# The first norm's roots on ScalarE, a memset put behind the head, a product ahead of beta's, and an order planned with instruction fetches, in a four-block attention and FFN kernel

## The chip, the cores and the metric

The kernel runs on one core of a Trainium2 chip. The metric is the device time of one execution in microseconds. The median of 3 runs of the kernel before is 536.74 us (536.57 to 538.55).

## What is computed

The input is 2048 tokens of 512 features in bf16. Four residual blocks follow each other: an infini-attention, a gated FFN, the same attention and the same FFN again, with the same weights in both rounds. Every block starts with a layer norm without weights.

```python
def _layernorm(x, axis=-1, eps=1e-05):
    m = jnp.mean(x, axis=axis, keepdims=True)
    v = jnp.var(x, axis=axis, keepdims=True)
    return (x - m) / jnp.sqrt(v + eps)

# attention: 32 heads of 16, the tokens in N = 4 segments of 512, per segment s
logits = jnp.einsum('bhqd,bhkd->bhqk', qs, ks) * scale + mask     # causal
a_dot = jnp.einsum('bhqk,bhkd->bhqd', _softmax(logits), vs)
pq = phi(qs)                                   # where(t > 0, t + 1, exp(t))
a_mem = einsum('bhld,bhde->bhle', pq, M) / (einsum('bhld,bhd->bhl', pq, z)[..., None] + 1e-06)
o = g * a_mem + (1.0 - g) * a_dot              # g = sigmoid(beta), per head
M = M + einsum('bhld,bhle->bhde', phi(ks), vs)
z = z + einsum('bhld->bhd', phi(ks))

# FFN, F = 1792
_gelu(x @ w_gate) * (x @ w_up) @ w_down

x = x + _A_ref(_layernorm(x), ...)     # then _B_ref, _A_ref, _B_ref
```

## The kernel before

**Tiling.** x stays in SBUF as 16 tiles of 128 tokens by 512 features. The work is cut into 8 steps, k = 0 to 7: four segments of 512 tokens in the first round and four in the second. Step k has an attention (class `Att`) and an FFN (class `Ffn`) on the same 512 tokens. An FFN of one step runs interleaved with the attention of the next, so that TensorE has dense products while ScalarE works off the exponentials. Step 0's attention has no FFN beside it; step 7's FFN has no attention beside it.

**One attention.** The norm makes `xn` (DVE, L670; on POOL now and then) from means and variances (L620/L623) and reciprocal roots (POOL, L651 adds eps, L657 raises to the power -0.5). `xn` is transposed to `xnT`, by a DMA from SP's queue (`turn_later`, L520) or by TensorE and an eviction (`turn_item`, L712 and L544/L545). Products make q, k (`kf`) and v. Heads lie 32 rows apart in pairs, so `kx` holds copies of k with one head of each pair masked to zero (`masked_copies`, L495/L500 and a DMA, L799). Scores go to PSUM (L1086), one exponential of 1024 columns at a time turns them into `pt` on ScalarE (L1589), causal masks follow on POOL or DVE (L1538, L1543, L1548), then a "flush" multiplies `pt` by v (L1115), and DVE transposes, normalises and transposes back (L1134, L1144, L1150, L1157) into `aT`. The product with `wo` is added to x (L1206). That sum feeds the FFN's norm, key `xnTf`, whose output feeds the gate products.

**Head of the program.** Lines 1362 to 1425 are written by hand: statistics of the four x tiles (three by BN_STATS on DVE, tile 3 by two ScalarE passes L1383/L1384), roots on POOL (L1378), `xn` (L670), 16 transposes on TensorE (L722) evicted by ScalarE (L725) and DVE (L727), beta's product and its two exponentials (L1408 to L1410), and the first block of k and q in halves of 256 tokens (`first_k` L1059, `first_q` L1064, evictions L1415 to L1424). Before that TensorE does 12 products on a constant tile (`keep_warm`, L417), and DVE zeroes half of one `kx` buffer (L448).

**What sets the order.** Behind the head, a planner written in Python (`order`, with `Clocks` and `Engine`) puts out every engine's instructions in one order. It holds an assumed time for each engine, assumed costs for each operation, and for DMAs an assumed landing time, `max(t + 1.4 + margin, ...)`, ahead of which nothing that needs the data is put out. Its choices (which engine evicts, when a product is due, how urgent a step is) come from a table of numbers, `POLICY`, and from `STAGES`, which changes the numbers per stretch of 20 us of planned time. Where the planner finds nothing ready for TensorE, it puts out a "fill": a product on the constant tile `warm`. On the chip each engine runs its own list in that order and waits on semaphores.

**Three forms of product.** TensorE is used as one 128x128 array ("whole", L559), as four strips of 32 columns (`product` with `tile_position=(0, 32 * c)`, L554; four matmuls for one product; flushes too have this form), or as four strips of rows (scores). The planner stays in a form as long as it can, since a change of form costs time.

**The steps of the FFN's norm (k = 0, 1, 7 are special).** `BY_PE` names the norms whose transposes go to TensorE: those of the FFNs of steps 0, 1 and 7. `QUICK` names the rows of step 1 where the sum with x and the squares are taken by one DVE pass and one ScalarE pass (L633 to L640). All other norms take the roots for four tiles at once and transpose by DMA.

## Time and profile before

| what | value |
|---|---|
| median of 3 runs | 536.74 us (536.57 to 538.55) |
| the profiled execution | 536.73 us |
| its span (first to last instruction) | 534.8 us |
| instructions in the span | 22313 |
| TensorE matmuls | 9803, busy 526.8 us |
| ScalarE | 544 instructions, busy 433.8 us |
| DVE | 814 instructions, busy 432.7 us |
| POOL | 344 instructions, busy 280.2 us |
| exponentials of the scores, L1589 | 288, 1032 ns each |

The profiled execution's time is 1.9 us longer than its span; the rest lies before the first and after the last instruction shown. PE stands for TensorE, ACT for ScalarE, DVE for VectorE, POOL for GpSimd, SP for the engine whose queue issues most DMAs. A row of a timeline has the start, the busy time, the engine, the line of the kernel, the operation with the tiles out<-in, a count, and in brackets how long the engine was idle before it and what released it. Timeline rows put neighbouring instructions of a group together, so two rows of one engine can overlap.

### The profile page before, as it was taken

The page shows a single profiled execution, that of the slowest core. Times are in us where ns is not written, and L with a number is a line of the kernel's source. Part 1 is how long each engine was busy: PE and PEld are TensorE (multiplying, and loading weights), DVE is VectorE, ACT ScalarE, POOL GpSimd, SP SyncE. Part 2 cuts the span into 40 slices and gives each one's busy share as a digit, 9 for nine tenths or more (in the row PEclk, how much of TensorE's full clock was granted, in tenths as well). Part 3 has the DMA queues.
Part 4 walks back from the last instruction along what each step waited for, and adds up shares of the span by engine and source line. Part 5 has one row for each costly group of instructions (what it writes and reads, how often), then busy time and mean ns, then how long its engine had stood idle before and what let it go on. Part 6 is the DMA issues. An engine that isn't in the chain of part 4 may idle for free.

```text
span 534.8 us, 22313 instructions
## 1 busy us (share of the span) xinstructions
PE 526.8 (99%) x9803; PEld 270.1 (51%) x9803; DVE 432.7 (81%) x814; ACT 433.8 (81%) x544; POOL 280.2 (52%) x344
## 2 busy tenths in 40 slices
PE   8999999999999999999999999999999999999997
PEld 4544454555545455545444554545555456545444
DVE  7898899899999998688897889888786797786342
ACT  5999999997998799998999899998879977820320
POOL 4876767385836587337671697816465254100000
PEclk9999999999999999999999999999999999999999
DMA  8345910640122143210130130220231003100001
GB/s 271 67 116 113 242 33 2 171 76 18 34 49 44 24 52 61 43 32 4 43 80 1 26 82 4 42 52 12 63 63 23 1 12 92 24 4 31 11 0 39
DMA packets 72403, 28.83 MB, mean 54 GB/s; under 512 B 56690, under 2 KB 72306, under 8 KB 72306
## 3 DMA queue, kind: packets, MB, share of 16 engines
q1 hardware_dynamic: 72016, 27.15, 23.5%
q8 instruction: 76, 1.25, 1.0%
q10 hardware_dynamic: 290, 0.26, 0.1%
q14 instruction: 21, 0.17, 0.1%
HBM read 9.70 MB, written 2.10 MB: 22 GB/s over the span
## 4 chain that ended last, share of the span: by engine, by line
PE 89%; DVE 5%; ACT 4%; issue 1%; POOL 1%; ACTq 0%; DVEq 0%; POOLq 0%
PE ps L559 43%; PE ps L554 30%; PE ps L1086 8%; PE ps L1115 6%; ACT pt L1589 2%; DVE st L620 1%; DVE gel_sb L1277 0%; ACT wd_sb L545 0%; PE ps L1015 0%; DVE x_sb L1206 0%; DVE byq L1134 0%; DVE e L894 0%; DVE st L1368 0%; DVE xn L670 0%; PE ps L712 0%
## 5 line engine op out<-in xcount | busy, mean ns | idle before, releaser
L1589 ACT ACTIVATE pt<-ps 128x1024 bf16<-128x1024 f32 x288 | 280.3, 1032 | 35.6 <-PE ps L1086 27.2
L1538 POOL TENSOR_SCALAR_AFFINE_SELECT pt<-pt 128x256 bf16<-128x256 bf16 (+1 forms) x192 | 113.9, 606 | 126.5 <-ACT pt L1589 123.1
L1277 DVE TENSOR_TENSOR gel_sb<-gel_sb,ps 128x512 bf16<-128x512 bf16 x112 | 75.6, 683 | 35.6 <-PE ps L559 25.3
L559 PE MATMUL ps<-xnT,wg_sb 128*128 128x512 bf16 x279 | 65.5, 380 | 0.0
L559 PE MATMUL ps<-xnT,wu_sb 128*128 128x512 bf16 x269 | 62.0, 379 | 0.0
L913 POOL TENSOR_SCALAR e<-e 128x512 bf16<-128x512 bf16 x37 | 58.0, 1569 | 2.6 <-ACT e L890 2.0
L1134 DVE STREAM_TRANSPOSE byq<-ps 128x512 f32<-128x512 f32 x64 | 45.3, 707 | 15.5 <-PE ps L1115 14.3
L559 PE MATMUL ps<-wd_sb,gel_sb 128*128 128x512 bf16 (+1 forms) x289 | 56.8, 347 | 0.0
L1206 DVE TENSOR_TENSOR x_sb<-x_sb,ps 128x512 bf16<-128x512 bf16 (+1 forms) x65 | 41.1, 641 | 19.1 <-PE ps L559 15.0
L554 PE MATMUL ps<-wd_sb,gel_sb 128*32 128x512 bf16 (+1 forms) x860 | 49.9, 368 | 0.2 <-issue 0.2
L1543 POOL TENSOR_SCALAR_AFFINE_SELECT pt<-pt 64x1024 bf16<-64x1024 bf16 x28 | 33.4, 1195 | 16.8 <-ACT pt L1589 15.8
L554 PE MATMUL ps<-xnT,wg_sb 128*32 128x512 bf16 x676 | 41.5, 380 | 0.2 <-ACT xnT L545 0.2
L554 PE MATMUL ps<-xnT,wu_sb 128*32 128x512 bf16 x716 | 41.1, 379 | 0.1
L559 PEld LDWEIGHTS <-wg_sb 128*128 128x128 bf16 x279 | 25.7, 98 | 29.7 <-issue 0.9
L559 PEld LDWEIGHTS <-wu_sb 128*128 128x128 bf16 x269 | 25.2, 98 | 29.8 <-issue 0.7
L620 DVE BATCH_NORM_STATS2 st<-x_sb 128x6 f32<-128x512 bf16 x57 | 38.4, 673 | 0.3
L559 PEld LDWEIGHTS <-gel_sb 128*128 128x128 bf16 x289 | 26.8, 98 | 23.2 <-issue 0.9
L1115 PE MATMUL ps<-pt,vaug 128*32 128x256 bf16 (+2 forms) x1344 | 34.8, 238 | 0.0
L544 DVE CAST gel_sb<-ps 128x512 bf16<-128x512 f32 x42 | 28.4, 681 | 6.7 <-PE ps L559 4.0
L1115 PEld LDWEIGHTS <-vaug 128*32 128x32 bf16 x1344 | 27.8, 97 | 10.5 <-issue 1.6
L1336 ACT ACTIVATE gel_sb<-gel_sb 128x2048 bf16<-128x2048 bf16 (+3 forms) x22 | 32.3, 1540 | 0.0
L1086 PEld LDWEIGHTS <-kx 32*128 32x128 bf16 x1120 | 16.6, 92 | 29.0 <-issue 28.4
(152 smaller groups left out, 871.6 us busy)
## 6 DMA issues: line engine op xcount, KB each, us to landing
vz<-vaug SPq DMA_DIRECT2D x14, 136.0 KB, 2.6
wg_sb<-in_B_w_gate_dram SPq DMA_DIRECT2D x8, 224.0 KB, 4.1
wu_sb<-in_B_w_up_dram SPq DMA_DIRECT2D x8, 224.0 KB, 6.4
wd_sb<-in_B_w_down_dram SPq DMA_DIRECT2D x7, 256.0 KB, 4.6
x_sb<-in_A_x_dram SPq DMA_DIRECT2D x3, 512.0 KB, 6.8
out_dram<-x_sb SPq DMA_DIRECT2D x12, 128.0 KB, 1.8
xnT<-xn SPq DMA_TRANSPOSE x48, 2.6
kx<-kf SPq DMA_DIRECT2D x12, 64.0 KB, 2.6
```

Of the source, the lines that this page charges most:

```text
L554: nc.tensor.matmul(out[r], lhsT=lhsT[:, r], rhs=rhs, start=start, stop=stop, tile_position=(0, 32 * c))
L559: nc.tensor.matmul(out, lhsT=lhsT, rhs=rhs, start=start, stop=stop)
L620: nc.vector.bn_stats(out=self.st6[:, 0, :], in_=x_sb[:, self.tt0 + j, :])
L913: lambda eng: eng.tensor_scalar(out=e[0][:], in0=e[0][:], scalar1=1.0, scalar2=None, op0=ALU.min), summed)
L1086: nc.tensor.matmul(ps_all[:, bank, o + c0:o + c0 + n], lhsT=lhsT, rhs=self.q[rows, b, q0:q0 + n], start=True, stop=True, tile_position=(32 ...
L1115: nc.tensor.matmul(ps()[32 * j:32 * j + 32, q0:q0 + nq], lhsT=va[:, ki * VW + g:ki * VW + g + 32], rhs=pt_all[:, places[t], j, o:o + nq], ...
L1134: nc.vector.transpose(out=(self.byq[:, pars[0], :, :].rearrange("p a c -> p (a c)") if h is None else self.byq[:].rearrange("p u a c -> p ...
L1206: ck.dve.post(ck.made(), slack, (0.15 + 0.00104 * (c1 - c0), lambda: nc.vector.tensor_tensor(out=xt, in0=xt, in1=ps()[:, 0:c1 - c0], op=AL ...
L1277: ck.dve.post(ck.made(), NORMAL, (0.683, lambda: nc.vector.tensor_tensor(out=g, in0=g, in1=ps()[:], op=ALU.mult), lambda t: (ps.read(t), e ...
L1538: nc.gpsimd.affine_select(out=view, in_=view, pattern=[[0, 4], [0, n], [1, C]], compare_op=ALU.is_ge, fill=0.0, base=C, channel_multiplier=-1)
L1543: nc.gpsimd.affine_select(out=view, in_=view, pattern=[[0, 4 * TPS], [1, C]], compare_op=ALU.is_ge, fill=0.0, base=0, channel_multiplier=-1)
L1589: nc.scalar.activation(out=pt_all[:, s0:s0 + 2, 2 * p:2 * p + 2, :].rearrange("p r h c -> p h r c"), in_=ps_all[:, pair[0]:pair[1] + 1, :] ...
```

## The change

It has four parts.

1. **The head.** ScalarE now sums and squares x tile 0 instead of tile 3. The reciprocal roots are made by ScalarE, `Ln` with eps as its bias and `Exp` with scale -0.5, for tiles 0 to 2 at once and for tile 3; the two adds of eps on DVE and the two powers on POOL go. A call loads the table set that has both functions. The memset of `kx` leaves the head and is handed to the planner as a job from 12 us on. The turns go to PSUM banks 0, 3, 5, 6, are evicted by ScalarE and DVE alternately, and have one 256-wide product on `warm` between two of them. The first half block of k comes ahead of beta's product, and beta's two exponentials come behind the evictions of the first k and q. The load of x tiles 4 to 7 comes ahead of the second halves of wk and wq.
2. **The norms.** The roots can go to POOL as before, or to ScalarE as `Ln` and `Exp`; the planner chooses. Roots may be taken for pairs of rows (`paired`). The tables `BY_PE` and `QUICK` are replaced by policy numbers (`turn_pe`, `turn_last`, `quick`, `f_urge`) for all FFN norms.
3. **The planner.** It counts TensorE's instructions (`Products`, `issue`) and adds a stall where a chunk of 256 of them would be used up before the next is there, 3.7 us after it was asked for. The landing of a DMA is modelled (`landing`) with a margin of 0.5 us instead of 2.0. Assumed overlaps of ACT and DVE and some assumed costs are new.
4. **The numbers.** `POLICY` is new, and `STAGES` has 13 entries instead of 3. Loads of weights get their times from it.

```diff
+CHUNK, CHUNK_ASKED, CHUNK_END, FETCH = 256, 178, 222, 3.7
...
-BY_PE = {("xnTf", 0), ("xnTf", 1), ("xnTf", NK - 1)}
-QUICK = {("xnTf", 1): (0, 1, 2)}
...
 POLICY = dict(
-    flush_wait=4.959, piece_slack=35.752, kb_slack=40.713, mem_slack=-52.285, margin=2.0, qk_due=1.503, e_q=-1.996,
...
+    rs_pool=2.183, f_urge=-172.366, quick=0, paired=2, turn_pe=1, turn_last=0, w_at=31.878, w_gap=1.658,
...
+    margin=0.5, qk_due=0.997, e_q=-0.936, e_k=1.44, exp_slack=-54.603, e_slack=89.377, phi_slack=25.941,
...
-        self.act, self.dve, self.pool, self.sp = Engine(0.09), Engine(0.07), Engine(), Engine()
+        self.act, self.dve, self.pool, self.sp = Engine(0.118), Engine(0.075), Engine(), Engine()
...
+    def issue(self):
+
+        at = self.issued
+        self.issued += 2.0054
+        if (at - CHUNK_ASKED) // CHUNK != (self.issued - CHUNK_ASKED) // CHUNK:
+            self.asked.append(self.pe)
+        elif (at - CHUNK_END) // CHUNK != (self.issued - CHUNK_END) // CHUNK:
+            late = max(0.0, self.fetched - self.pe)
+            self.stalls += [self.pe] * int(late / 0.05)
+            self.pe += late
+            self.fetched = self.asked[-1] + FETCH if self.asked else 0.0
+
+    def landing(self, t):
+
+        got = max(t + 1.2, self.dma + 1.2)
+        for a in self.asked[-3:]:
+            if -0.6 < a + 1.1 - t < 1.1:
+                got = max(got, a + 2.3 + (1.5 if a + 1.1 < t + 0.1 else 1.1))
+        return got
...
-load_x(1)
+        if not cols.start:
+            load_x(1)
...
-    nc.vector.memset(kxs[1][:, :, :, C:3 * C], 0.0)
...
+    ck.dve.post(12.0, pol.zero_slack, (Port(0.95), lambda: nc.vector.memset(kxs[1][:, :, :, C:3 * C], 0.0),
+                                       lambda t: ev.update({("zero", 1): t})))
...
     def turn_later(t, slack, out, in_, landed, margin=0.0):
 
+        def there(t2):
+            t3 = ck.landing(t2) + margin
+            ck.at(t3 - 0.2, lambda: landed(t3))
+
         def told(t2):
-            t3 = max(t2 + 1.4 + margin, ck.dma + 1.2)
-            ck.at(t3 - 0.2, lambda: landed(t3))
+            ck.at(t2, lambda: there(t2))
...
+            def moved(on_pool):
+                self.ve = wrk.tile([P, n, 1], F32, tag=f"lnve{n}", name="ve")
+                var_in = self.mv[:, j0:j0 + n, var:var + 1]
+                if on_pool:
+                    nc.gpsimd.tensor_scalar(out=self.ve[:], in0=var_in, scalar1=EPS_LN, scalar2=None, op0=ALU.add)
+                else:
+                    nc.scalar.activation(out=self.ve[:], in_=var_in, func=ACT.Ln, bias=eps[:])
...
+            taken = []
+            slack = min(self.urge(j0), URGENT)
+            ck.pool.post(ready, slack + pol.rs_pool, (0.25, lambda: moved(True), None), (1.05, second, told), taken=taken)
+            ck.act.post(ready, slack, (0.29, lambda: moved(False), None), (0.29, power, told), table="exp", taken=taken)
...
         def by_pe(self):
-            return self.key in BY_PE or self.key[0] == "xnTa" and self.key[1] <= pol.pe_turns
+            return (pol.turn_last if self.key[1] == NK - 1 else pol.turn_pe) if self.wide else self.key[1] <= pol.pe_turns
...
     def first_scale(j0, j1):
-        nc.gpsimd.tensor_tensor(out=n0.rs[:, j0:j1, :], in0=n0.mv[:, j0:j1, 1:2], in1=mhalf[:, 0:j1 - j0, :], op=ALU.pow)
+        nc.scalar.activation(out=logs[:, j0:j1, :], in_=n0.mv[:, j0:j1, 1:2], func=ACT.Ln, bias=eps[:])
+        nc.scalar.activation(out=n0.rs[:, j0:j1, :], in_=logs[:, j0:j1, :], func=ACT.Exp, scale=-0.5)
...
+    for j in range(TPS):
+        n0.first_turn(j)
+        if j < TPS - 1:
+            keep_warm(1, 4, 2)
...
+    a0.first_k(ps1, 0, half)
+    te.matmul(beta_ps, lhsT=warm[0:1, :], rhs=beta_row[:], start=True, stop=True)
+    a0.first_q(ps2, 0, half)
...
-    ck.pe, ck.act.free, ck.dve.free, ck.pool.free, ck.sp.free = 10.6, 11.1, 11.0, 8.1, 7.6
+    ck.pe, ck.act.free, ck.dve.free, ck.pool.free, ck.sp.free = 9.3, 9.9, 9.95, 8.0, 7.6
```

Since the planner sets the order, the diff doesn't show where instructions go. Three places follow, with the rows of the engine's list before and after.

The first is DVE's list in the head. `kx` is the buffer that is zeroed, `st` and `mv` are the statistics, `xn` is the normed tile. Before:

```order
L448 MEMSET kx_121 128x16x64
L1368 BN_STATS st_144<-x_sb 128x6
L1368 BN_STATS st_145<-x_sb 128x6
L1371 BN_AGGR mv<-st_144 128x2
L1371 BN_AGGR mv<-st_145 128x2
L1374 TENSOR_SCALAR mv<-mv 128x2
L1368 BN_STATS st_146<-x_sb 128x6
L1371 BN_AGGR mv<-st_146 128x2
```

And of the change, from the same place on:

```order
L1501 BN_STATS st_145<-x_sb 128x6
L1501 BN_STATS st_146<-x_sb 128x6
L1504 BN_AGGR mv<-st_145 128x2
L1504 BN_AGGR mv<-st_146 128x2
L1501 BN_STATS st_147<-x_sb 128x6
L1522 TENSOR_SCALAR mv<-shift 128x1
L1504 BN_AGGR mv<-st_147 128x2
L801 TENSOR_SCALAR xn<-x_sb,mv,rs 128x512 x4
```

The memset and the adds of eps are gone from between the loads and `xn`, and the four `xn` stand together.

The second is DVE's list between the first attention and its FFN: the last sums with x (L1206, now L1338), their statistics, and `xn` for the FFN's norm, to which TensorE's transposes and the first gate products belong. Before:

```order
L1206 TENSOR_TENSOR x_sb<-x_sb,ps 128x512
L620 BN_STATS st_1618<-x_sb 128x6
L623 BN_AGGR mv<-st_1618 128x2
L620 BN_STATS st_1634<-x_sb 128x6
L623 BN_AGGR mv<-st_1634 128x2
L1134 STREAM_TRANSPOSE byq<-ps 128x512
L894 SCALAR_TENSOR_TENSOR e,zk<-wd_sb,e 128x512
L544 CAST vaug_140<-ps 128x16x2x16
L670 TENSOR_SCALAR xn<-x_sb,mv,rs 128x512 x4
```

And of the change:

```order
L740 BN_AGGR mv<-st_1585 128x2
L737 BN_STATS st_1697<-x_sb 128x6
L740 BN_AGGR mv<-st_1697 128x2
L1338 TENSOR_TENSOR x_sb<-x_sb,ps 128x512
L801 TENSOR_SCALAR xn<-x_sb,mv,rs 128x512
L737 BN_STATS st_1735<-x_sb 128x6
L740 BN_AGGR mv<-st_1735 128x2
L801 TENSOR_SCALAR xn<-x_sb,mv,rs 128x512
L1175 COPY macc<-ps 128x128
L1266 STREAM_TRANSPOSE byq<-ps 128x512
L659 COPY xnT<-ps 128x4x128
L801 TENSOR_SCALAR xn<-x_sb,mv,rs 128x512 x2
```

The roots of the first two rows are used before the last row has its statistics, and a transpose, a value eviction and a step of the memory's sum (`e,zk`) no longer stand between the last statistics and the first `xn`.

The third is ScalarE's list at the end, where the norm of the last FFN lies (`xnT` is its transposed output, `gel_sb` the gelu's). Before:

```order
L1336 ACT_TABLE_LOAD
L1336 ACTIVATE gel_sb<-gel_sb 128x2048
L1253 ACTIVATE gel_sb<-ps 128x512 x4
L1336 ACTIVATE gel_sb<-gel_sb 128x2048
L1336 ACTIVATE gel_sb<-gel_sb 128x1024
L545 ACTIVATE xnT<-ps 128x4x128 x2
L1239 ACTIVATE gel_sb<-ps 128x512 x14
```

And of the change:

```order
L1468 ACTIVATE gel_sb<-gel_sb 128x512 x8
L464 ACT_TABLE_LOAD
L757 ACTIVATE junk,mv<-x_sb,mv 128x512
L777 ACTIVATE ve<-mv,eps 128x2
L783 ACTIVATE rs<-ve 128x2
L777 ACTIVATE ve<-mv,eps 128x2
L783 ACTIVATE rs<-ve 128x2
L1371 ACT_TABLE_LOAD
L1371 ACTIVATE gel_sb<-ps 128x512 x14
```

ScalarE now loads the exponentials' table between the two gelu stretches, takes one square pass and both pairs of roots, and loads gelu's table again; the evictions of `xnT` are gone, since the transposes of this norm are now four DMAs from SP's queue.

282 lines of the change are left out of this document (179 added, 103 removed).

## The prediction

> **What bounds the kernel now.** I read the page first, for the engines' shares and the chain of work that ended last, and then the span cut into stretches.
>
> ```profile
> span 534.8 us, 22313 instructions
> PE 526.8 (99%) x9803; PEld 270.1 (51%) x9803; DVE 432.7 (81%) x814; ACT 433.8 (81%) x544; POOL 280.2 (52%) x344
> PE 89%; DVE 5%; ACT 4%; issue 1%; POOL 1%; ACTq 0%; DVEq 0%; POOLq 0%
> core 0: us, PE busy (x) PEld busy (x) DVE busy (x) ACT busy (x) POOL busy (x), PEclk, DMA share, GB/s
> 0.00:10.00 10.00, 8.40 (x45) 4.13 (x45) 7.13 (x23) 4.86 (x11) 3.63 (x15) 1.00 0.81 250
> 20.00:40.00 20.00, 18.68 (x430) 9.97 (x422) 18.93 (x42) 19.18 (x27) 15.85 (x20) 1.00 0.54 112
> 60.00:80.00 20.00, 19.09 (x436) 10.37 (x435) 18.86 (x42) 18.48 (x25) 15.41 (x18) 1.00 0.55 110
> 260.00:340.00 80.00, 80.00 (x1590) 39.98 (x1583) 70.71 (x129) 73.96 (x92) 51.23 (x58) 1.00 0.16 34
> ```
>
> TensorE bounds it, at full clock, with 89% of the chain. From 260 to 340 us it has no gap at all: an order can gain there only by taking work from TensorE. Gaps are where it waits: 1.3 us of 20 to 40 and 0.9 of 60 to 80. ScalarE is nearly full from 20 to 40 us (19.18 of 20). So I take three stretches: up to the first gate product, the rest, and the tail. My sums are made against the profiled execution, 536.73 us, which is 0.01 below the median of the runs, so they need no shift.
>
> **Head.** These are the timeline's rows from the first statistics to the first scores.
>
> ```profile
> 2.80 0.91 DVE L448 MEMSET kx<- 128x1024 uint32 x1 [0.16 <-issue]
> 3.63 1.22 DVE L1368 BATCH_NORM_STATS2 st<-x_sb 128x6 f32<-128x512 bf16 x2
> 6.44 0.79 POOL L1378 TENSOR_TENSOR rs<-mv,mhalf 128x2 f32<-128x2 f32 x1 [0.31 <-DVE mv L1374]
> 7.27 0.73 DVE L670 TENSOR_SCALAR xn<-x_sb,mv,rs 128x512 bf16<-128x512 bf16 x2 [0.21 <-POOL rs L1378]
> 7.74 0.72 PE L722 MATMUL ps<-ident,xn 128*128 128x128 bf16 x8 [0.17 <-DVE xn L670]
> 8.22 0.22 ACT L1410 ACTIVATE tmp_e<-ps 128x32 f32<-128x32 f32 x1
> 10.38 0.40 PE L1086 MATMUL ps<-wd_sb 16*128 16x256 bf16 x12 [0.17 <-DVE tmp_e L464]
> ```
>
> Without the memset the statistics start when the tiles are there and DVE is free of the small work ahead of it, some 0.2 us sooner. They can't gain the memset's whole 0.91, since the tiles have to land too, and three BN_STATS still run in a row (1.22 for the first two). A power on POOL takes 0.79 us and an add of eps on DVE stands ahead of it; a small ScalarE exponential (32 columns) takes 0.22, so I price Ln and Exp together at 0.43 and the two pairs at 0.86, where the second power ends at 7.23 now. That puts the last transposes about 0.5 us ahead of 7.74; three 256-wide products on the constant tile go between them, in time in which TensorE waited anyway. I take **0.4 us** off the first scores (10.38), between 0 and 0.8. The load of x tiles 4 to 7 passes the second halves of wk and wq on SP's queue: 512 KB at the 250 GB/s of the first 10 us make those 2.1 us later, but the products up to the first scores use the first halves alone. The memset comes back as 0.91 us on DVE before 20 us, behind the first block's evictions; ahead of it DVE takes statistics, and what it delays is the eviction of the next q, a part of the bounds at the wall.
>
> [...] No trace here shows an Ln yet.
>
> **The wall in front of the first gate product.** The next rows are the exponentials up to the end of the first attention's scores, the transposed `aT`, and the chain from it through the FFN's norm to the first gate product; then the fills.
>
> ```profile
> L1589 ACT ACTIVATE pt<-ps 128x1024 bf16<-128x1024 f32 x36 | 34.8, 1060 | 1.4 <-PE ps L1086 0.8 <-POOL kx L495 0.4 <-POOL pt L1538 0.2
> L500 ACT ACTIVATE kx<-kf,masks 128x256 bf16<-128x256 bf16 x2 | 1.1, 546 | 0.0
> L890 ACT ACTIVATE e<-wd_sb 128x512 bf16<-128x512 bf16 x1 | 0.7, 654 | 0.0
> 54.48 1.94 ACT L1589 ACTIVATE pt<-ps 128x1024 bf16<-128x1024 f32 x2 [0.16 <-PE ps L1086]
> 60.89 0.71 DVE L1157 STREAM_TRANSPOSE aT<-ab 128x512 bf16<-128x512 bf16 x1
> 63.30 0.68 DVE L1206 TENSOR_TENSOR x_sb<-x_sb,ps 128x512 bf16<-128x512 bf16 x1
> 69.43 0.18 DVE L623 BATCH_NORM_AGGREGATE mv<-st 128x2 f32<-128x6 f32 x1
> 69.70 0.23 POOL L651 TENSOR_SCALAR ve<-mv 128x4 f32<-128x4 f32 x1 [1.57 <-DVE mv L623]
> 70.01 1.04 POOL L657 TENSOR_TENSOR rs<-ve,mhalf 128x4 f32<-128x4 f32 x1
> 71.77 1.43 DVE L670 TENSOR_SCALAR xn<-x_sb,mv,rs 128x512 bf16<-128x512 bf16 x4
> 73.33 1.01 PE L712 MATMUL ps<-ident,xn 128*128 128x128 bf16 x15
> 75.58 1.18 ACT L545 ACTIVATE xnT<-ps 128x512 bf16<-128x512 bf16 x2
> 76.81 0.40 PE L554 MATMUL ps<-xnT,wg_sb 128*32 128x512 bf16 x4 [0.16 <-ACT xnT L545]
> L559 PE MATMUL ps<-warm 128*128 128x128 bf16 x15 | 2.3, 219 | 0.3 <-ACT pt L1589 0.2
> L554 PE MATMUL ps<-warm 128*32 128x128 bf16 x60 | 2.1, 222 | 0.3 <-ACT wd_sb L545 0.2
> ```
>
> Before, the way from `aT` (61.60) to the gate product (76.81) takes 15.2 us. With the change, the rows are: 1.7 us from `aT` to the first sum as now (63.30 less 61.60), four sums at 0.67 and four statistics at 0.87 (0.69 and 0.18) on DVE, 6.2 us; then one pair of roots on ScalarE, 0.43; two `xn` at 0.36, 0.7; four transposes and an eviction, about 0.3 and 0.6. That is 9.9, or 5.3 us less; I take 5.1, since a `macc` copy, a transpose of the next attention and ScalarE's exponentials (1.06 us each, in order) can come between. Against it stands more ScalarE work ahead of the wall. The change's list has, up to the 36th exponential, five more masked copies of k (mean 0.55 to 0.7, say 0.6: 3.0 us), two more `e` exponentials (1.3), one more eviction (0.65) and one pair of roots (0.43): 5.4 us. ScalarE's gaps among those 36 are 1.4 us; half of that can take some of the work, and the head gives 0.4. So the last exponential comes 5.4 - 0.7 - 0.4 = 4.3 us later, and the first gate product comes 5.1 - 4.3 = **0.8 us** sooner. The bounds: 2.5 us sooner, if POOL's masked copies (the releaser of 0.4 us of gaps) were what delayed the scores and the extra copies on ScalarE bring them forward; 1.0 later, if `aT` comes that much later and the chain saves only 3.3. The list of TensorE shows the same from the other side: fills are 12 early and 7 at the wall before, none early and 21 at the wall after. Each counts 0.22 us or less, so the two are near to even.
>
> **Products behind it.** The transposes by TensorE go from 64 to 48; 16 of them at the 56 ns that a 128-wide product keeps TensorE (its 220 ns are a pipelined duration) are 0.9 us. The list has 299 changes of form before and 296 after, at about 0.1 us as the trace's starts show: 0.3 us. More products are in column form (the list has 10462 matmuls for 9803), but a product costs TensorE the same in either form: 112 column matmuls, 28 products of 512 columns, took 6.22 us (row in the tail's fence), 0.22 each, and whole ones start 0.216 us apart. So 1.2 us of work go; half lies ahead of the gate, in waits counted above, and I take **0.6** (0 to 1.0).
>
> **Waits behind the gate.** Here are rows where TensorE or its weight loads stood for "issue", and where it waited for ScalarE.
>
> ```profile
> 37.31 0.53 PEld L559 LDWEIGHTS <-wk_sb 128*128 128x128 bf16 x3 [0.29 <-issue]
> 132.67 0.29 PE L1086 MATMUL ps<-q,kf 16*128 16x64 bf16 x6 [0.38 <-ACT pt L1589]
> 161.39 0.55 PEld L554 LDWEIGHTS <-wu_sb 128*32 128x32 bf16 x15 [0.24 <-issue]
> 174.87 1.04 PE L554 MATMUL ps<-wd_sb,gel_sb 128*32 128x512 bf16 x13 [0.22 <-issue]
> 454.60 0.10 PEld L1086 LDWEIGHTS <-kx 32*128 32x128 bf16 x4 [0.25 <-issue]
> ```
>
> From starts against their normal spacing I count 2.75 us of waits behind 76.8 us; 11 fills stand there, which cost 0.056 us each, 0.6. Together 3.3. After the change the list has 9 fills there; each stands where nothing was ready, and at a fill's duration of 0.22 us (219 ns in the row above) that is 2.0 us of waits: **1.3 us less**, between 3.3 (all waits go) and -2 (waits of the same kind come up at places that the planner doesn't see, as the four "issue" rows did).
>
> The rows at 37, 161, 175 and 455 are waits for nothing that the profile shows; from the starts they cost 0.18, 0.31, 0.59 and 0.29, together 1.4 us. [...]
>
> **Tail.** The last FFN's norm changes most, so its cover has to be named.
>
> ```profile
> 463.68 1.28 ACT L1336 ACT_TABLE_LOAD   x1
> xnT<-xn SPq DMA_TRANSPOSE x48, 2.6
> wg_sb<-in_B_w_gate_dram SPq DMA_DIRECT2D x8, 224.0 KB, 4.1
> 482.39 6.22 PE L554 MATMUL ps<-wd_sb,gel_sb 128*32 128x512 bf16 x112
> 519.70 12.29 PE L559 MATMUL ps<-wd_sb,gel_sb 128*128 128x512 bf16 x70
> ```
>
> A DMA transpose lands 2.6 us behind its issue. From the last `wo` product to the first gate product come a sum, a square or statistics, a table load (1.28), roots, two `xn`, and four transposes that SP issues one after the other: 0.7 + 0.9 + 1.3 + 0.4 + 0.7 + 2.6 = 6.6 us, or 7.9 with another issue of 1.3 us ahead of the last. Down products of the FFN before cover it, 56 products of 0.216 us = 12.1 us (6.22 for the first 28 of them now). So it costs **nothing**; without the cover it would be 6.6 to 7.9. Gelu's second table load, 1.28, runs while the gate products do. Roots and squares elsewhere lie beside a full TensorE (260 to 340) and cost nothing while ScalarE has its 6 us of slack there.
>
> **Sum.** -0.8 - 0.6 - 1.3 = -2.7 us: 536.73 - 2.7 = **534.0 us**.
>
> **Rivals.** (A) Everything goes as the planner means it: the wall falls by 2.5, 0.9 of products, and all of 2.75 us of waits but a fill or two: 536.7 - 4.5 to 7 = 529.7 to 532.2. For it speaks that the last 350 us already run without gaps, so that little can go wrong there. Against it: 21 fills still stand at the wall. (B) The order gives back what the head gains: waits with nothing named come at new places (1.4 us again; the list has 659 more matmuls, each with a weight load, so 5 more chunks of 256), and the wall is even or up to 1.0 later. Then only the transposes remain of the gain: 535.3 to 537.5. That is also the case in which the counting of fetches doesn't do what it is meant to. For it speaks that the planner's idea of TensorE's time has to be right to a few tenths of a microsecond over 500 us, against it that just these waits are what it now counts. (C) Slower: transfers land later than planned. In the planner an issue takes SP 1.34 us; before, nothing that needs the data was put out until 3.4 us behind that (4.7 from the issue's start), now until 1.7 behind (3.0). The median landing is 2.6 us from the issue, so the slack shrinks from 2.1 to 0.4 us. 100 transposes and 28 stores pass SP's queue, with TensorE's list in order behind each of them: a late `xnT` or `phik` stops it. Where a transfer takes 4.1 us, as the gate weights' do on the same queue, the stop is 1.1 us; the mechanism decides from five such stops on that don't fall into fills: 534.0 + 5.5 = 539.5, and with eight 542.8.
>
> **How the numbers follow.** My forecast, 532.2 to 535.3, has 0.40; A 0.25; B 0.20; C 0.15. The range holds my forecast and B whole, reaches to the upper half of A and up to C's edge: 530.0 to 538.5, which also takes in the bounds of the unknown costs (at the wall -2.5 and +1.0, in the waits -3.3 and +2). A measurement of this kernel can tell about 0.5%, 2.7 us, from no change: below 534.06 is faster, above 539.4 slower. Half of my forecast and all of A lie below: 0.20 + 0.25 = 0.45 for faster. The other half and B make 0.40 for no change, and C 0.15 for slower.
>
> **What would show it.** The wall: the first gate product by 76.0 us, the first scores by 10.0, the 36th exponential near 60.7 (56.42 before). If the gate product is later than 77.8, my size of ScalarE's extra work or of the chain is wrong. Waits: rows with "issue" at PE or its loads behind 77 us add to less than 0.5 us if the fetch model is right; the same 1.4 us at other places is B. C shows as PE rows released by a DMA, on `xnT`, `phik` or `amT`. Tail: the first gate product of the last FFN comes right behind the last down product, with no idle time; more than 1 us there makes my nothing wrong. A DVE or ScalarE that releases TensorE again and again between 180 and 460 us would make the whole prediction wrong.

## The result, and the profile after

The change is slower: 538.34 us (median of 11 runs, 537.38 to 539.38) against 536.72 for the kernel before (median of 11 runs on the same chip, 536.16 to 538.55). The ratio is 1.0026, with an interval of 1.0014 to 1.0038. The prediction was 534.0; the time is 4.3 us above it. Taken again on another chip, the ratio is 1.0040 [1.0027, 1.0052]. These 1.6 us lie below the 0.5% named in the prediction, so in its terms the outcome is "no change", but the interval leaves 1.0 out. Four executions among all those behind this document (600 us of the kernel before, and 755, 876 and 883 us of three others) ran at mean clocks of 0.56 to 0.85 and are in no ratio here.

The profiled execution took 537.38 us, the fastest of the 11. Its trace lacks 59 matmul records, so stretches and waits of TensorE are shown from the second profile of the same kernel (537.55 us, nothing missing). First the page of the change: span, busy time and the chain of waits.

```profile
span 535.7 us, 23633 instructions
PE 518.7 (97%) x10403; PEld 272.4 (51%) x10462; DVE 438.7 (82%) x834; ACT 438.9 (82%) x589; POOL 275.2 (51%) x343
PE 85%; DVE 9%; issue 2%; ACT 2%; DMA 0%; POOL 0%; DVEq 0%; POOLq 0%
```

And the span in stretches, from the second profile (columns as in the prediction: busy time of each engine, granted clock, DMA).

```profile
20.00:40.00 20.00, 19.54 (x370) 9.66 (x372) 17.19 (x39) 20.00 (x29) 16.80 (x24) 1.00 0.62 89
40.00:60.00 20.00, 20.00 (x420) 10.21 (x418) 17.18 (x32) 19.52 (x26) 13.96 (x18) 1.00 0.83 209
60.00:80.00 20.00, 18.66 (x414) 10.30 (x406) 19.66 (x42) 18.66 (x24) 14.09 (x19) 1.00 0.59 139
260.00:340.00 80.00, 80.00 (x1651) 40.72 (x1647) 72.94 (x147) 67.65 (x90) 52.45 (x58) 1.00 0.27 47
```

TensorE still has no gap from 260 to 340. From 20 to 40 it gained 0.9 us of busy time (18.68 before), and from 60 to 80 it lost 0.4 (19.09 before). So waiting was moved from one stretch into another.

**Head.** The timeline of the change, from the first statistics to the first transposes, and the first scores:

```profile
3.47 1.29 DVE L1501 BATCH_NORM_STATS2 st<-x_sb 128x6 f32<-128x512 bf16 x2 [0.79 <-DMA x_sb<-in_A_x_dram]
5.24 0.30 ACT L1507 ACTIVATE logs<-mv,eps 128x3 f32<-128x3 f32 x1
5.56 0.20 ACT L1508 ACTIVATE rs<-logs 128x3 f32<-128x3 f32 x1
6.13 0.20 ACT L1508 ACTIVATE rs<-logs 128x1 f32<-128x1 f32 x1
6.27 0.40 PE L426 MATMUL ps<-ident,xn 128*128 128x128 bf16 x4 [0.66 <-DVE xn L801]
6.95 0.39 PE L426 MATMUL ps<-ident,xn 128*128 128x128 bf16 x4
7.28 0.39 PE L426 MATMUL ps<-ident,xn 128*128 128x128 bf16 x4
10.37 0.40 PE L422 MATMUL ps<-wd_sb 16*128 16x256 bf16 x12
```

The statistics now wait for the x tiles (0.79 us for a DMA) and start 0.16 us sooner than before. The prediction's row at 7.74 is the transposes of the last two tiles, eight of them; these now start at 6.95 and end at 7.67 (8.46 before), 0.8 us sooner, where 0.5 were foreseen. But the first scores start at 10.37, where they stood at 10.38: TensorE has more products in front of them (two of 512 columns for q that came behind them before). The sooner start went into products, not into the scores.

**The wall.** The rows of the change that answer to the prediction's: the 36th exponential (the end of the first row), `aT`, and TensorE up to the first gate product.

```profile
57.56 1.97 ACT L1716 ACTIVATE pt<-ps 128x1024 bf16<-128x1024 f32 x2
64.38 0.71 DVE L1289 STREAM_TRANSPOSE aT<-ab 128x512 bf16<-128x512 bf16 x1
65.15 1.47 PE L422 MATMUL ps<-wo_sb,aT 128*128 128x512 bf16 x6 [0.22 <-DVE aT L1289]
70.90 0.35 PE L422 MATMUL ps<-warm 128*32 128x128 bf16 x12 [0.43 <-DVE x_sb L1338]
73.22 0.27 PE L422 MATMUL ps<-warm 128*128 128x128 bf16 x2 [0.17 <-DVE byq L1266]
74.59 0.63 PE L422 MATMUL ps<-pt,vaug 128*32 128x256 bf16 x24 [0.54 <-POOL pt L1665]
76.35 0.27 PE L422 MATMUL ps<-warm 128*128 128x128 bf16 x2 [0.29 <-ACT xnT L660]
76.47 1.02 PE L422 MATMUL ps<-xnT,wg_sb 128*128 128x512 bf16 x3
```

`aT` ends at 65.09 (61.60 before), and the way from it to the gate product takes 11.4 us (15.2 before). The chain is 3.8 us shorter, `aT` is 3.5 us later, and the gate product comes 0.34 us sooner.

**Waits behind it.** Five of the largest, of TensorE and of its weight loads, from the second profile:

```profile
109.71 0.40 PE L422 MATMUL ps<-q,kx 32*128 32x256 bf16 x10 [0.42 <-ACT pt L1716]
116.42 0.40 PE L422 MATMUL ps<-q,kf 16*128 16x256 bf16 x12 [0.23 <-DVE x_sb L1338]
135.75 0.38 PE L422 MATMUL ps<-xnT,wg_sb 128*128 128x512 bf16 x1 [0.46 <-ACT xnT L660]
101.34 0.10 PEld L422 LDWEIGHTS <-wu_sb 128*32 128x32 bf16 x4 [0.19 <-issue]
124.01 0.55 PEld L422 LDWEIGHTS <-aT 128*32 128x32 bf16 x15 [0.21 <-issue]
```

**Where TensorE's time went.** I took every product's start against the next one's, in both first profiles (a missing record is put between its neighbours), and split the time into what the products stream, changes of form, waits, and fills:

```
us                        before    after   difference
useful streaming          483.76   482.68   -1.08
changes of form            30.04    30.42   +0.38
waits, whole program       12.40    12.69   +0.29
  of them behind 77 us      4.64     5.32   +0.68
fills                       4.30     4.63   +0.33
last product starts       531.71   531.66   -0.05
from there to the end       3.13     4.01   +0.88
```

The work that goes away is there, 1.1 us of it, and it is given back in waits, changes of form and fills: the last product starts where it did. What is new stands behind the last product. These are SP's last events in both traces (start in us; the last store of the output is issued at 532.47 and 532.43):

```
                                     before   after
last store has landed                533.99   534.11
SP's next wait on a DMA counter      534.01   534.13
four further waits on counters         none   534.19 to 534.41
first and second DRAIN               534.07, 534.13   534.48, 534.85
last event                           534.77   535.61
```

SP ends the program by waiting for its eight DMA counters in a fixed order. Before, the last store lies on the last one waited for; in the change it lies on the fourth, and the other waits, at 0.06 us each, and a gap of 0.37 us between two DRAINs come behind the landing. From landing to end of span: 0.84 us before, 1.56 after.

This covers most of what lies between the fastest runs (537.38 against 536.16). The medians lie further apart because of a second thing: the trace's granted clock of TensorE, averaged over the span, is 0.995 to 0.998 in seven of the change's eleven runs; in the runs of the kernel before beside the experiments it is 0.999 or 1.0.

### The profile page after: what moved, and what is told of

Read it like the earlier page. It is cut to its first block, busy times and chain, and to the rows that moved or that the text cites. A ratio compares the mean times of both kernels' runs of the same rounds, so it can differ in the third digit from the quotient of the medians.

```text
span 535.7 us, 23633 instructions
## 1 busy us (share of the span) xinstructions
PE 518.7 (97%) x10403; PEld 272.4 (51%) x10462; DVE 438.7 (82%) x834; ACT 438.9 (82%) x589; POOL 275.2 (51%) x343
## 4 chain that ended last, share of the span: by engine, by line
PE 85%; DVE 9%; issue 2%; ACT 2%; DMA 0%; POOL 0%; DVEq 0%; POOLq 0%
PE ps L422 84%; ACT pt L1716 2%; DVE byq L1266 1%; DVE x_sb L1338 1%; DVE e L1026 1%; DVE ab L1282 1%; DVE st L737 1%; DVE pt L1675 1%; DMA x_sb<-in_A_x_dram 0%; PE ps L426 0%; DVE gel_sb L1409 0%; DVE r L1276 0%; DVE aT L1289 0%; DVE st L1501 0%; DVE vaug L659 0%
## 5 line engine op out<-in xcount | busy, mean ns | idle before, releaser
L422 PE MATMUL ps<-xnT,wg_sb 128*32 128x512 bf16 (+1 forms) x1143 | 105.6, 380 | 2.0 <-issue 1.1
L422 PE MATMUL ps<-wd_sb,gel_sb 128*32 128x512 bf16 (+2 forms) x1486 | 102.4, 353 | 1.8 <-issue 1.6
L422 PE MATMUL ps<-xnT,wu_sb 128*32 128x512 bf16 (+1 forms) x1188 | 100.8, 379 | 1.3 <-issue 1.1
L422 PEld LDWEIGHTS <-gel_sb 128*32 128x32 bf16 (+1 forms) x1689 | 53.5, 97 | 40.8 <-issue 1.5
L422 PEld LDWEIGHTS <-wu_sb 128*32 128x32 bf16 (+1 forms) x1198 | 44.6, 97 | 46.9 <-issue 0.9
L422 PEld LDWEIGHTS <-wg_sb 128*32 128x32 bf16 (+1 forms) x1156 | 43.0, 97 | 42.8 <-issue 0.7
L1338 DVE TENSOR_TENSOR x_sb<-x_sb,ps 128x512 bf16<-128x512 bf16 (+1 forms) x59 | 37.1, 639 | 20.5 <-PE ps L422 19.7
L1468 ACT ACTIVATE gel_sb<-gel_sb 128x512 bf16<-128x512 bf16 (+4 forms) x42 | 35.3, 928 | 0.0
L422 PE MATMUL ps<-xnT,wq_sb 128*32 128x512 bf16 (+2 forms) x261 | 34.3, 377 | 0.8 <-issue 0.5
L422 PE MATMUL ps<-xnT,wk_sb 128*32 128x512 bf16 (+2 forms) x263 | 33.4, 376 | 1.0 <-issue 0.5
L422 PE MATMUL ps<-q,kx 32*128 32x64 bf16 (+2 forms) x1120 | 31.1, 217 | 0.5 <-ACT pt L1716 0.4
```

The costliest lines, as they stand in the source:

```text
L422: self.nc.tensor.matmul(*args, **kw)
L1338: ck.dve.post(ck.made(), slack, (0.15 + 0.00104 * (c1 - c0), lambda: nc.vector.tensor_tensor(out=xt, in0=xt, in1=ps()[:, 0:c1 - c0], op=AL ...
L1468: return (0.205 + 0.427 * (f1 - f0), lambda: nc.scalar.activation(out=g, in_=g, func=ACT.Gelu_apprx_tanh), lambda t: self.gelu_done(t, f0, ...
```

## The experiments

Two questions were taken first: which of the two parts of the change, head or order, costs the time, and whether the end is a matter of its tail. All edits are against the change unless it says "before". Every set has runs of the kernel before on the same chip, medians 536.77 to 536.95.

**The change again** (no edit).

> The changed kernel once more, unchanged. In its first profile TensorE's last product starts at 531.66 us (531.71 before), and the span is 0.84 longer for what follows the last product. Theory 1, the order costs what it costs each time: the median is again 1.0 to 2.0 us above before, 537.4 to 539.0, and a second profile shows stalls at the same places as the first to within 0.1 us. Theory 2, most of the difference is chance from execution to execution (transfers and instruction fetches that land late now and then): stalls of 0.3 us and more come at other places than in the first profile, and the runs spread by 2 us.

539.0 us (537.55 to 539.9), ratio 1.0040 [1.0027, 1.0052], with clocks from 0.995 to 1.0. Behind the gate the trace has the same waits at the same places; ahead of it two of the first trace's, at 65.15 and 74.59, are missing. The loss is the program's, not one chip's.

**The new head in the old order.** In before, the head's statements are those of the change:

```diff
-        nc.gpsimd.tensor_tensor(out=n0.rs[:, j0:j1, :], in0=n0.mv[:, j0:j1, 1:2], in1=mhalf[:, 0:j1 - j0, :], op=ALU.pow)
+        nc.scalar.activation(out=logs[:, j0:j1, :], in_=n0.mv[:, j0:j1, 1:2], func=ACT.Ln, bias=eps[:])
+        nc.scalar.activation(out=n0.rs[:, j0:j1, :], in_=logs[:, j0:j1, :], func=ACT.Exp, scale=-0.5)
...
-    nc.vector.memset(kxs[1][:, :, :, C:3 * C], 0.0)
```

> The kernel before with the new head alone (statistics, roots by ScalarE, transposes with products between, first k ahead of beta's product, x tiles 4 to 7 loaded earlier, memset of kx right behind the head); behind the head the order of every engine is that of before, instruction for instruction. Theory 1, what the head gains is lost by the first scores or by the wall, because the chain of ScalarE's exponentials starts no sooner (10.82 before, 11.27 in the changed kernel): within 0.3 us of before, first exponential 10.6 to 10.9. Theory 2, the head's 0.9 us of TensorE time carry through to the end: 0.6 to 1.0 us faster than before, and then the whole loss of the change lies in the new order.

536.49 us, ratio 0.9995 [0.9986, 1.0004]. By the medians the head alone gains 0.4 us, and by the interval perhaps nothing. In its profiled execution nothing came sooner: DVE waited 0.96 us for the second of the x tiles that it takes, the first transposes start at 7.28 (6.74 before), the first scores at 10.97 (10.38), and the first exponential at 11.41, outside the 10.6 to 10.9 expected. In that execution (536.99 us, 0.5 above the median) the landing of an x tile set the head's time.

**The old head in the new order** (the reverse edit, but for the order of the loads and the table load, which stay as in the change).

> The changed kernel with the head of before (statistics, powers on POOL, beta's product in the middle, memset of kx in the head, no products between the transposes); behind the head the order of every engine is that of the changed kernel, except that the memset is gone from it. Theory 1, the wall takes up whatever the head gives: within 0.4 us of the changed kernel. Theory 2, the head is worth 0.9 us: 0.6 to 1.0 us slower than the changed kernel.

538.58 us, ratio 1.0032 [1.0020, 1.0044]. The order carries the loss. Its profile has one wait for nothing named of 1.1 us at 148, where the change has 0.2 at 147: the same list of products, shifted by three products in the head, meets what I take for an instruction fetch at another place:

```profile
148.18 0.81 PE L422 MATMUL ps<-xnT,wq_sb 128*128 128x512 bf16 x3 [1.10 <-issue]
```

**The last FFN's down products whole**, 420 TensorE instructions fewer near the end, to see if an instruction fetch is what lengthens the end.

```diff
-        if ck.mode == "columns" or ck.mode == "rows" and (any(it.kind == "flush" and it.near() for it in items)):
+        if not plain and (ck.mode == "columns" or ck.mode == "rows" and (any(it.kind == "flush" and it.near() for it in items))):
```

> The changed kernel with the down products of the last FFN as whole products instead of four column strips each: 420 instructions fewer for TensorE at the end, the rest of the order the same. Theory 1: the 0.84 us that the changed kernel takes longer behind its last product come from a fetch of TensorE's instructions at 531.66 us that lies on the way of the output stores (the store issued at 530.90 lands at 533.94, 3.0 us later, against 1.5 before). Without those instructions the fetch isn't needed: no fetch behind 520 us, that store lands within 1.7 us, and the kernel is 0.6 to 0.9 us faster than the changed one. Theory 2, the late landing is chance: no change in the median (within 0.3 us).

538.05 us, ratio 1.0033 [1.0021, 1.0046]; from the last landing to the end it is 1.56 us as in the change. So my theory of the fetch fell. But its profiled execution was the slowest of its eleven (541.25 us, mean clock 0.993) and shows the clock. TensorE in short stretches (busy time, instructions, granted clock, DMA share, GB/s):

```profile
70.00:74.00 4.00, 3.38 (x130) 1.00 0.99 303
74.00:76.00 2.00, 0.91 (x34) 0.72 0.35 116
76.00:77.00 1.00, 1.00 (x41) 0.50 0.14 40
80.00:81.00 1.00, 1.00 (x15) 0.50 0.00 0
81.00:82.00 1.00, 1.00 (x4) 0.64 0.00 0
82.00:84.00 2.00, 2.00 (x24) 1.00 0.00 0
```

At the end of the wall TensorE runs at half clock from 74.9 to 81.7 us, 6.8 us: the gate products, which wait for nothing any more, start 427 ns apart and not 216. Two rows of the wall:

```profile
71.83 0.35 PE L422 MATMUL ps<-warm 128*32 128x128 bf16 x12 [0.44 <-DVE x_sb L1338]
75.77 1.04 PE L422 MATMUL ps<-pt,vaug 128*32 128x256 bf16 x24 [0.81 <-POOL pt L1665]
```

The longest wait of all, 0.9 us from start to start, is the one before 75.77 and lies behind the fall. Ahead of the fall no wait is over 0.6 us (the one before 71.83); between the waits stand fills of 128 columns, which follow each other 56 ns apart, while the planner sets aside 216 ns, the time of 512 columns, for each. From 71.4 to 74.9 us TensorE is busy for 2.6 of 3.5 us. The change's second profile has the same thin stretch at a clock of 1.00, so it lets the clock fall in some executions and not in others. The length of the fall differs too: 6.8 us here, and in the trace of the change with the end on another counter (below) 0.50 for 3.4 us, from 74.7 to 78.1. No idle gap of that length stands ahead of the fall here, only a stretch thin in work; what in it lets the clock fall, this trace doesn't show.

**Fills 512 columns wide**, so that the array streams through the wall.

```diff
-                product(ps()[:, 0:P], warm[:], wide[:, 0, :])
+                product(ps()[:, 0:L], warm[:], wide)
```

> The changed kernel with every fill 512 columns wide instead of 128 (30 fills; the planner already counted them with the time of 512 columns); the order stays the same. Theory 1: in one run of a sister kernel the granted clock was 0.50 from 75 to 81 us, behind the wall of fills and waits at 62 to 78 us, and 7 of 11 runs of the changed kernel had a mean clock below 0.999, where before had 1.0; with wider fills TensorE is busy enough there that the clock holds: all runs at 1.0 (0.999 at the least), median 537.2 to 537.8, 0.8 to 1.6 us faster than the changed kernel, and a spread below 1 us. Theory 2, the clock falls for another reason (or the wide fills hold up the products behind them): clocks as before, median 538 to 539.5.

538.35 us, ratio 1.0029 [1.0019, 1.0039]. All eight runs have a clock of 0.999 or 1.0. Over all kernels here that keep the change's order behind the head, 28 of 72 executions with fills of 128 columns have a mean clock of 0.998 or less, and none of 29 with 256 or 512; so it is the thin fills that let the clock fall there. But a wide fill holds up the work that comes ready behind it: the gate product comes at 77.13, the last product starts at 532.25, both some 0.6 us later, and nothing is won.

**The end on another counter.** The first tile's last store is cut in five, so that the stores behind it move on and the last one falls on the eighth counter again.

```diff
+                    if k == NK - 1 and j == 0:
+                        for d0, d1 in ((0, 128), (128, 256), (256, 384), (384, 448), (448, 512)):
+                            ck.sp.post(t, URGENT, (0.5, lambda d0=d0, d1=d1: load(
+                                of[:, self.tt0 + j, d0:d1], x_sb[:, self.tt0 + j, d0:d1]), None))
```

> The changed kernel with the output store of the first tile of the last step split into five, so that four more transfers are issued ahead of the last one; nothing else moves. Theory 1: behind the last landing the changed kernel takes 1.56 us to the end of the span and before 0.84, since SP waits for its eight transfer counters in a fixed order and the last store is on the fourth of them (on the eighth before); with four more it is on the eighth again: 0.9 us from the last landing to the end, and 0.4 to 0.8 us faster than the changed kernel in spans at clock 1.0 (lowest time 536.7 to 537.0). Theory 2, what takes longer is not the order of the waits but what follows (an instruction fetch, the drain): at most 0.3 us faster.

537.99 us, ratio 1.0016 [1.0007, 1.0025]; the fastest run, 536.71, is 0.67 below the change's fastest. From the landing (535.49) to the end (536.34) it is 0.85 us again. So the end is mended; how much of it is the counter itself, the next run tells.

**The same cut in before**, which moves its last store from the eighth counter to the fourth.

> The kernel before with the same split of the store of the first tile of the last step: the last store moves from the eighth counter to the fourth. Theory 1: 0.4 to 0.8 us slower than before, 1.3 to 1.6 us from the last landing to the end of the span. Theory 2: within 0.3 us of before.

536.93 against 536.95, ratio 1.0005 [0.9996, 1.0014]. From the landing to the end 1.10 us, 0.26 more than before: the four waits are there, the gap between the DRAINs (0.07 us here) is not. So the waits cost 0.26, too little for the medians to show, and the other 0.46 us of the change's end (1.56 less 1.10) lie in and behind a DRAIN whose delay stays unexplained. Eight traces with the last store on the fourth counter have 0.36 to 0.38 us between the DRAINs; the run with a margin of 2.0 us (below) has the last store on that counter too and 0.06. The counter alone doesn't make that gap. The added stores also move everything behind them in SP's list, and which of the two takes the 0.46 us away isn't shown.

**Wide fills and the end together.**

> Both edits in the changed kernel: wide fills and four more stores. If theory 1 holds for both, the median is 536.5 to 537.2, level with before within 0.4 us: then the clock and the end are the whole of the measured loss, and the new order itself is neither better nor worse. If it stays above 537.8, a part of the loss lies in the order.

537.94 us, ratio 1.0022 [1.0013, 1.0031], all clocks 1.0. By the expectation this leaves a part of the loss in the order. I put it down to the wide fills' own price, but its trace also has an instruction fetch that holds TensorE up for 1.7 us near 63.9, so the two aren't told apart here.

**Masked copies of k on DVE** up to 60 us, to free ScalarE, which the prediction took for the reason of the late `aT`.

```diff
+            if ck.pe < 60.0:
+                return vector(which, nc.vector)
```

> The changed kernel with the eight masked copies of k that ScalarE makes ahead of 60 us (0.5 to 0.75 us each, 4.9 us in all) made by DVE at the same places of the program (0.26 to 0.33 us each); everything else keeps its order. Theory 1: the wall in front of the first gate product is set by ScalarE's chain, which the change made 3.1 us longer up to the 36th exponential (59.53 us, 56.42 before), mostly with these copies. Then the 36th exponential ends 2 to 4 us sooner, the first gate product comes at 73.5 to 75.5 instead of 76.47, TensorE's waits at 60 to 77 us fall by 1.5 to 3 us, the clock holds more often, and the kernel is 1.5 to 3.5 us faster than the changed one (median 535 to 537). Theory 2, the wall is set by the norm's chain on DVE or by TensorE's own work, so that ScalarE only waits earlier: first gate product within 0.5 us of 76.47, time within 0.5 us of the changed kernel.

538.37 us, ratio 1.0034 [1.0018, 1.0051]. With eight copies fewer on ScalarE, the 36th exponential ends at 60.08 and not sooner than 59.53: from 10 to 60 us ScalarE is busy 46.2 us instead of 49.1, and waits 2.8 us for scores instead of 0.8. ScalarE's load was not what set the wall. TensorE is full from 40 to 60 us, and its list sets the scores. The first gate product comes at 77.87, 1.4 us later than in the change. What came in between is another fetch wait, here on one product:

```profile
62.54 0.29 PE L422 MATMUL ps<-pt,vz 128*32 128x64 bf16 x15
63.83 0.20 PE L422 MATMUL ps<-pt,vz 128*32 128x64 bf16 x1 [1.01 <-issue]
```

At that place, in one and the same order of products, the wait is 0 in the change's first profile, 0.2 in its second, 0.5 with the end on another counter, 0.8 with the whole down products, 1.2 here and 1.7 with wide fills and the end together. The traces record the reads of instructions, 16 KB each; the change's second has 82 of them for 20924 weight loads and products of TensorE, one for every 255. Here one starts at 61.48, among the loads of `wu`, and the product starts 2.35 us behind it; in the five others with a wait the distance is 2.3 to 2.5 us (the fifth has fills of 256 columns). In the first profile the read starts at 58.87 and nothing waits. So how long the product waits follows from how late the read starts.

**The same with the end's cut.**

> The same, with the split store of the first tile of the last step, which took 0.7 us off the end of the span (0.85 us behind the last landing instead of 1.56). Theory 1 for both: 534.5 to 536.3, faster than before by 0.5 to 2 us. If the copies bring nothing: 537 to 538, as the split store alone.

537.81 us, ratio 1.0018 [1.0008, 1.0027]: only the end's part comes back.

**No stall in the planner for a fetch.**

```diff
-            late = max(0.0, self.fetched - self.pe)
+            late = 0.0
```

> The changed kernel's planner with the stall for instruction fetches set to zero: it plans another order from some place on (PE's list differs in length by 258 rows), with the same table of numbers. Theory 1, the counting of fetches does what it is meant to: more rows with TensorE or its loads idle for nothing named behind the first gate product than the changed kernel's 101, 124, 147 and 447 us (0.18 to 0.3 us each, 0.9 together), 1.5 us or more together, and a slower kernel by 0.5 to 2 us. Theory 2, the model doesn't hold on the chip, waits of that kind only move: 0.6 to 1.2 us of them, and the time moves with the order by up to 2 us either way, whatever the reason.

550.08 us, ratio 1.0252 [1.0235, 1.0269].

**A margin of 2.0 us for landings.**

```diff
-    margin=0.5, qk_due=0.997, e_q=-0.936, e_k=1.44, exp_slack=-54.603, e_slack=89.377, phi_slack=25.941,
+    margin=2.0, qk_due=0.997, e_q=-0.936, e_k=1.44, exp_slack=-54.603, e_slack=89.377, phi_slack=25.941,
```

> The changed kernel's planner with a margin of 2.0 us behind the assumed landing of a transfer instead of 0.5, as before; again another order with the same table. Theory 1, the short margin costs waits for late transfers, which the first profile of the changed kernel doesn't show (no row of TensorE released by a DMA behind the first gate product): then the time falls by 0.5 to 1.5 us and the spread at clock 1.0 with it. Theory 2, the margin isn't at fault: slower by 0.5 to 3 us, because a longer margin leaves more places where nothing is ready, with a table tuned for the short one.

553.9 us, ratio 1.0326 [1.0304, 1.0348]. Both kernels have another order throughout, and their waits lie everywhere. The waits of the first one's TensorE, by releaser (total, times, longest):

```profile
PE ps L422 <- DVE x_sb L1338: 2.5, 4, 1.1
PE ps L422 <- ACT pt L1716: 2.3, 6, 0.5
PE ps L422 <- issue: 1.4, 2, 0.7
```

These two don't measure what the fetch model or the margin is worth. Both edits move the whole order, and both cost 13 to 17 us against before; the table of numbers seems to fit one trajectory of the planner alone. So experiments have to hold the order fixed, as the others here do.

**The fetches moved, the order held.** 32 small products (with their weight loads 64 instructions) in the head, in time in which TensorE waits.

```diff
+    for _ in range(32):
+        nc.tensor.matmul(ps_all[:, 0, 0:8], lhsT=warm[:], rhs=wide[:, 0, 0:8], start=True, stop=True)
```

> The changed kernel with 32 products of 8 columns in the head, in a gap of 0.8 us where TensorE waits for the first normed tile: 64 more of TensorE's instructions (32 weight loads, 32 products), so that every fetch of its instructions falls a quarter of a block of 256 sooner in the order, which stays the same. Theory 1, the planner's fetch model is worth something, because it knows where the fetches fall: with them elsewhere, waits for nothing named come up at new places, 1 to 3 us more behind 77 us than in the changed kernel, and the time is 0.7 to 3 us longer. Theory 2, where the fetches fall matters little for this order: within 0.5 us of the changed kernel (538.3 to 539), waits at other places but no more of them.

540.3 us, ratio 1.0062 [1.0047, 1.0077], above the change's own 1.0026 and 1.0040 by 1.9 and 1.2 us, though the interval overlaps that of the second. The profile shows a new wait in the middle of four transposes:

```profile
72.43 0.28 PE L426 MATMUL ps<-ident,xn 128*128 128x128 bf16 x2
74.04 0.29 PE L426 MATMUL ps<-ident,xn 128*128 128x128 bf16 x2 [1.33 <-issue]
```

The read of instructions starts at 71.61, 2.4 us ahead of the late transposes. Where such a read falls relative to the work is worth over a microsecond in this kernel (the 1.33 us above), with every product in its place. Most of the 82 reads in the change's second trace hold nothing up; those in all traces that do cost 0.2 to 1.7 us each. The long ones ahead of 75 us stand in a busy DMA (a share of 0.95 from 72 to 73 us here), but the 1.1 us near 148 with the old head stand where the share is 0.03, so a busy DMA isn't the whole reason.

**The last FFN's transposes by DMA in before**, the part of the change's tail that the prediction priced at nothing.

```diff
-BY_PE = {("xnTf", 0), ("xnTf", 1), ("xnTf", NK - 1)}
+BY_PE = {("xnTf", 0), ("xnTf", 1)}
```

> The kernel before with the norm of the last FFN transposed by four DMAs instead of 16 TensorE transposes; up to there the order is that of before, behind it the tail's products are in column strips (the form isn't changed back) and the last store moves from the eighth counter to the fourth (0.26 us, as measured). By my prediction's terms: 16 transposes at 56 ns, 0.9 us less for TensorE, and nothing for the chain, which 12 us of down products cover: 536.77 - 0.9 + 0.26 = 536.1 (535.8 to 536.4). If the cover fails: TensorE idle ahead of the last FFN's first gate product, 537 or more. If the end of the span grows by 0.7 as in the changed kernel: 536.5.

538.44 us, ratio 1.0033 [1.0021, 1.0045]: a loss of 1.5 us.

**The same with the new head and the end's cut.**

> The kernel before with the new head and the DMA transposes of the last norm, and the split store of the first tile of the last step, which brings the last store back to the eighth counter. If the parts add up (head -0.3 as measured, transposes -0.9, end 0): 535.3 to 535.9, faster than before by 0.9 to 1.5 us and faster than both kernels. If one of them only works alone: 536.2 to 536.8.

537.53 us, ratio 1.0012 [1.0003, 1.0020]. In both, TensorE stands for the last of the four transposes. This is the one with the new head:

```profile
489.70 4.74 PE L556 MATMUL ps<-wd_sb,gel_sb 128*32 128x512 bf16 x140
495.92 1.91 PE L556 MATMUL ps<-xnT,wg_sb 128*32 128x512 bf16 x32 [1.47 <-DMA xnT<-xn]
```

The fourth transpose is issued at 491.45 and lands at 495.67, 4.2 us later, where the three ahead of it take 2.4. In the change itself the cover holds. One of the four takes 4.2 us there too (issued at 487.13, landed at 491.35), but it is the second (and 3.5 us for the third); they are issued from 485.84, the last has landed at 493.19, and the gate products follow the down products without a gap (the first two rows are TensorE's, the last is SP's queue).

```profile
491.76 3.88 PE L422 MATMUL ps<-wd_sb,gel_sb 128*32 128x512 bf16 x124
495.46 2.77 PE L422 MATMUL ps<-xnT,wg_sb 128*32 128x512 bf16 x48
...
485.84 6.13 SPq L635 DMA_TRANSPOSE xnT<-xn  x4
```

**Fills of 256 columns and the end's cut**: half-way, to hold the clock without holding up work.

```diff
-                product(ps()[:, 0:P], warm[:], wide[:, 0, :])
+                product(ps()[:, 0:2 * P], warm[:], wide[:, 0:2, :])
```

> The changed kernel with fills of 256 columns (128 in the changed kernel, 512 in the wide one) and the split store. Theory 1, half the width holds the clock and holds up less: clocks 0.999 to 1.0, median 537.0 to 537.6. Theory 2, what is left above before lies in the order: 537.7 to 538.2 as with 512 columns.

537.44 us (lowest 536.36), ratio 1.0005 [0.9996, 1.0014], clocks 0.999 and 1.0. Level with before: the end and the clock together are the whole loss that can be measured, though the interval leaves room for up to 0.75 us more in the order. TensorE around the wall, in the columns of the stretches above:

```profile
74.00:78.00 4.00, 2.75 (x79) 1.00 0.21 69
78.00:82.00 4.00, 4.00 (x80) 1.00 0.00 0
```

From 74 to 78 us it waits more than the change's second profile does (busy 2.75 us against 3.70), and keeps its clock. No kernel here beats before by more than its interval.

## Why the prediction was wrong

It forecast 534.0 and left slower by over 0.5% a chance of 0.15. The time came inside its rather wide range but on the other side of no change. By its own steps:

- **Head, -0.4 us for the first scores: measured 0.0.** The last two tiles' transposes were 0.8 us sooner, where 0.5 had been worked out (a pair of roots takes 0.30 + 0.20 = 0.50 us, against 0.43 assumed). The time was taken by products ahead of the scores. With the old order behind it, the head brought the scores no sooner either, since an x tile landed late in that trace.
- **Wall, -0.8: measured -0.34, for another reason than the one given.** The chain from `aT` fell by 3.8 us instead of 5.1; `aT` came 3.5 later instead of 4.3. The two misses, 1.3 us too much and 0.8 too much, mostly cancel; that the step came out with the right sign is luck. The cause I named, ScalarE's extra copies, fell with the copies moved to DVE. What the lists and stretches show in its place, not tried by itself: TensorE is full from 40 to 60 us, and the new order places more dense products ahead of the scores there. At 45 us' worth of useful streaming the change is 3.3 us ahead of before; at 60 us' worth it is level again (78.2 against 78.1). The products brought forward are those that could have filled the wall, where waits and fills now take 4.7 us (2.0 before). A lead in work is not a lead in time, if the stretch it feeds is bound by a chain.
- **Products behind it, -0.6: measured -0.7.** Useful streaming falls by 1.27 us behind 77, and 0.54 goes to more changes of form. The size is right; the sign of the form term was not (I had it at -0.3 over the whole program, it is +0.38).
- **Waits behind the gate, -1.3: measured +0.7. This step failed.** It took the planner's fills for the waits to come, at a duration of 219 ns each where their starts lie 56 ns apart, and the fetches for the part that the new model removes. The waits at which nothing is named went only from 1.19 to 0.95 us (161, 175 and 455 before, as the prediction counted them; 101, 124, 147 and 447 after), above the 0.5 that I had set as the mark of a working model. That mark lumped two things together: by the recorded reads of instructions only 175 and 455 before stand 2.6 and 2.4 us behind a read, as the fetch waits of the experiments do, and after the change only 147 does, 2.8 us, in the first trace alone. So the fetch waits, 0.9 us of them, mostly went, as the model meant; the others at which nothing is named came up at new places. Those for other engines grew: of the ones over 0.15 us, 1.04 before (108, 132, 388) and 2.2 after (109, 116, 135, 149, 207 and 360, for `pt`, `x_sb`, `xnT` and `gel_sb`). This is rival B, in a stronger form: the waits moved, and the gain of the products was given back. That waits for other engines would grow is what the step left out.
- **Tail, nothing: the named chain did cost nothing, but the tail's four DMAs cost at the end.** The cover of the norm held, as the rows of the last FFN show. It was thinner than the sum of 6.6 to 7.9 against 12.1 us made it: in before's order, where the transposes come some 2 us later, a last landing of 4.2 us instead of 2.6 opens a wait of 1.5 to 1.9. What I did not count is that four more DMAs turn the counters, so that the last store lands on one that SP doesn't wait for last: +0.7 us at the end, of which 0.26 are the waits and 0.46 belong to a DRAIN whose cause is open.
- **The clock: not in the sum at all.** I took it for full because it is 1.00 in every row of before. The wall of the change, with more fills and waits together, lets it fall in most runs. Of the change's 17 executions on both chips, the seven at 0.999 or 1.0 have a median of 537.75 and the ten others of 538.88. The median with the end mended is 1.1 parts in a thousand, 0.6 us, above the one with wider fills too.
- **Rival C did not come.** No product behind the head waits for a DMA in the change's trace, with a smaller margin than before. In one other trace of its order, the copies on DVE with the end's cut, one does: 0.61 us at 70.31, for `phik`.

The sum as measured in the two first profiles, by TensorE: -0.05 at the last product, +0.88 behind it. My estimate for the medians, from the runs above: end 0.7, clock about 0.6 (538.34 less 537.75), and 0.3 that the runs don't tell from nothing.

## What to carry to other kernels

When a planned order is exchanged for another, price it by what bounds each stretch: products brought forward from a stretch that is waiting on a chain are no gain. Look at what a change does to everything that is counted in turn, the DMA counters at the program's end and the reads of instructions among them: four more DMAs moved the last store to another counter here, with 0.26 us (before) and 0.7 us (the change) more at the end, and 64 more instructions moved a fetch to where it cost 1.33 us. Where TensorE is kept busy with small fills, look at the granted clock of many runs and not of one profile, and try wider ones: here 256 columns, half of the 512 whose time the planner sets aside for a fill, kept the clock at 0.999 or 1.0 in all eleven executions compared.
